# Attention with the fifth blocks of two heads in one transpose, 1/sum spread by transposes, and reordered maxima, products and table loads, in front of two gated layers on one core

## The chip, the cores and the metric

One core of a Trainium2 chip runs the whole program. The metric is device time in microseconds (us) of one execution; the programs are the kernel before the change and the kernel after it. The engines are named as the profile names them: PE (matmul) with PEld (its weight loads), DVE (vector), ACT (scalar activation), POOL (GpSimd), SP (which here only issues DMAs).

## The reference

Attention with rotated q and k over 2 batches, 8 heads, 576 positions and 64 dimensions, then two layers over 1152 tokens of 512, each with a hidden width of 2048, the first with ELU, the second with x·tanh(softplus(x)).

```python
q_rot, k_rot = (rotate(q), rotate(k))
scores = scale * np.matmul(q_rot, k_rot.transpose(0, 1, 3, 2))
scores = scores - np.max(scores, axis=-1, keepdims=True)
attn = np.exp(scores)
attn = attn / (np.sum(attn, axis=-1, keepdims=True) + 1e-09)
return np.matmul(attn, v).astype(np.float32)
...
h = x @ w_in
g = np.where(h > 0.0, h, alpha * (np.exp(np.minimum(h, 0.0)) - 1.0))
return (g @ w_out).astype(np.float32)
...
h = x @ w_in
sp = np.where(h > 20.0, h, np.log1p(np.exp(np.minimum(h, 20.0))))
g = h * np.tanh(sp)
return (g @ w_out).astype(np.float32)
```

## The kernel before

The 16 heads are handled as 8 pairs of heads, both heads of a pair side by side in the 128 partitions. A pair has nine score tiles of 128 query rows by 576 keys: tile i = 0..7 is head i mod 2, query rows 128·(i div 2) and on, and tile 8 holds the last 64 query rows of both heads. One step of the main loop is a unit u = 9p + i, and the order in which the loop body calls its parts is the order in each engine's queue (the schedule is by hand). The stages of a unit are spread over later units:

- `do_S` (L385): the scores into the double bank `ps_s` (two buffers), as products of values split into a rounded high part and a rest. In pairs 0 and 1 (`FLAT = 2`) the two heads of a double tile (units u and u+1, u even within the pair) are multiplied together in rows 0-63 and 64-127, and all of it is issued in the even unit. From pair 2 on each tile has its own four matmuls with stacked operands `ka`, `qa`, `qb`, which POOL splits (L298, L299) and SP copies into place (L323) during the pair before.
- `do_max` (L392, DVE) the row minimum of the negated scores; `do_exp` (L400, ACT) exp into the tile `P` (four buffers) with the row sum accumulated aside.
- `do_T`, three units later (`LAG`): four transposes of 128x128 into one of two banks `psT` (L441) and a fifth of the last 64 keys into `psL` (L442); `do_evac` (L455 on DVE, L457 on ACT) and `do_evac_last` (L467, DVE) bring them to `pt`, a tile with the five key chunks.
- `do_inverse` (L409 to L418, DVE): 1/sum of a group of tiles (group 0 is tiles 0 to 3, 256 query columns; group 1 is tiles 4 to 8, 320 columns), each widened to 64 columns; `do_spread` (L423, PE) turns it into a row layout in the bank `psA` by fp32 products with the identity; `do_keep` (L432, ACT) copies it to `R`.
- `do_av` (L473): five key chunks; in each, head 0 goes to output partitions 0-63 of `psA` and head 1 to 64-127, in fp32, which is two records per matmul in the trace. `do_x` (L488, DVE) multiplies by `R` and frees `psA`; `do_xh`, `do_xl` split the result into `XH` and `XL`, the operands of the first layer.

A table `plan` says in which unit each spread and product stands: the spread of group 0 in unit 6 of a pair, its products in units 7 and 9, the spread of group 1 in unit 11 (unit 2 of the next pair), its products in units 12 and 14. POOL rotates q and k of the pair after next (L273 to L277), and weights of the first layer are prepared in the last pairs (`weight_part`). After the last tile, `tail` puts first-layer products (L183, `g1_mm`) between the remaining steps. The layers that follow are a stream of matmuls on PE (L183, L683, L712).

In what follows, stage 1 is units 0 to 17 (pairs 0 and 1), stage 2 the units from 18 to 70, stage 3 the rest of attention with its tail, stage 4 the two layers. What one double tile does in stage 1, on each engine's queue, is

```python
do_S(u)            # even unit: both tiles
do_max(u)
do_T(u - LAG)
do_spread / do_av
do_evac(u - LAG)
do_exp(u)
```

so in the old order the maximum of tile u+1 stands on DVE behind the work of unit u.

## Time and profile before

| | us |
|---|---|
| runs, median of 3 | 574.96 |
| lowest, highest | 574.5, 1397.33 |
| the profiled execution's own time | 570.46 |
| its span, first to last instruction | 568.6 |

The profile is of one execution, so its rows add up to its own time, which is 4.5 us below the median. PE is busy 97% of the span and the granted clock is full (1.00) throughout. A row of the timeline gives the start within the span, the length, the engine, the line of the kernel, the operation, what it writes and reads, the shape, how many instructions were merged, and in brackets the engine's idle time before it and what ended it. The ends of matmuls are modelled, so the cost of a PE instruction in a dense stretch is read from start to start.

### The profile page before, as it was taken

The numbers are of one execution on the slowest core, as the hardware profiler recorded it, in microseconds if no ns is written. First come the engines' busy times: TensorE is split into PE (matmuls) and PEld (weight loads), VectorE is DVE, ScalarE is ACT, GpSimd is POOL, SyncE is SP. The second block draws the span as 40 slices with busy tenths as digits, with TensorE's granted clock in tenths as the row PEclk, the third lists the DMA queues.
The fourth block names the chain that finished last, engine by engine and source line by source line (L and its number), as shares of the span: only waits on it lengthen the run. The fifth ranks groups of instructions, "written<-read, shape, count | busy, mean of one in ns | idle before, by whom it ended". The sixth has DMA issues, their size and how long they took to land.

```text
span 568.6 us, 10131 instructions
## 1 busy us (share of the span) xinstructions
PE 553.9 (97%) x3888; PEld 499.7 (88%) x3888; DVE 376.9 (66%) x607; ACT 277.9 (49%) x512; POOL 238.7 (42%) x227
## 2 busy tenths in 40 slices
PE   7799999999999999999999999999999999999997
PEld 6568677777789999999999999999999998999985
DVE  6666899888846766777777777869844555432222
ACT  3646666667755665455555456435443322322110
POOL 6998999982310323323322331445533332230000
PEclk9999999999999999999999999999999999999999
DMA  6368676655110323223222322234532423000012
GB/s 231 110 197 258 205 228 178 184 143 161 38 39 4 108 80 107 76 76 96 91 74 78 108 75 75 85 115 139 159 116 84 121 88 110 22 14 10 29 65 93
DMA packets 43120, 60.69 MB, mean 107 GB/s; under 512 B 13760, under 2 KB 31936, under 8 KB 42304
## 3 DMA queue, kind: packets, MB, share of 16 engines
q1 hardware_dynamic: 42528, 59.46, 34.2%
q8 instruction: 31, 0.51, 0.4%
q10 hardware_dynamic: 544, 0.59, 0.3%
q14 instruction: 17, 0.14, 0.1%
HBM read 46.20 MB, written 2.36 MB: 85 GB/s over the span
## 4 chain that ended last, share of the span: by engine, by line
PE 85%; DVE 6%; ACT 3%; DMA 2%; issue 1%; POOL 1%; SPq 1%; ACTq 0%; POOLq 0%; DVEq 0%
PE ps_s L183 34%; PE ps_g L683 18%; PE ps_h L712 17%; PE ps_s L385 5%; PE psA L473 5%; PE psT L441 4%; DMA qk_t<-in_qk_dram 2%; PE psA L423 2%; DVE mn L392 1%; ACT P L400 1%; DVE wu L99 1%; PE psL L442 1%; DVE pt L455 1%; DVE R L488 0%; DVE rw L411 0%
## 5 line engine op out<-in xcount | busy, mean ns | idle before, releaser
L392 DVE TENSOR_REDUCE mn<-ps_s 128x1 f32<-128x576 f32 x72 | 53.9, 751 | 19.2 <-PE ps_s L385 15.2
L661 ACT ACTIVATE ta<-ps_s 128x576 f32<-128x576 f32 x32 | 20.8, 649 | 92.7 <-PE ps_s L183 92.6
L400 ACT ACTIVATE P<-ps_s,mn 128x576 f32<-128x576 f32 x72 | 53.1, 739 | 9.5 <-DVE mn L392 6.8
L183 PE MATMUL ps_s<-XH,wi0h 128*128 128x288 f32 x256 | 54.9, 296 | 0.9 <-DVE tb L218 0.9
L99 DVE TENSOR_SCALAR wu<-wu 128x512 int32<-128x512 int32 x64 | 33.7, 527 | 32.9 <-POOL wu L95 32.9
L183 PE MATMUL ps_s<-XL,wi0h 128*128 128x288 f32 x256 | 54.5, 294 | 0.0
L183 PE MATMUL ps_s<-XL,wi1h 128*128 128x288 f32 x256 | 54.4, 294 | 0.0
L183 PE MATMUL ps_s<-XH,wi0l 128*128 128x288 f32 x256 | 54.4, 294 | 0.0
L183 PE MATMUL ps_s<-XH,wi1l 128*128 128x288 f32 x256 | 54.2, 293 | 0.0
L183 PE MATMUL ps_s<-XH,wi1h 128*128 128x288 f32 x256 | 54.1, 293 | 0.0
L122 POOL TENSOR_TENSOR wi1l<-wu,wi1h 128x512 fp32r<-128x512 f32 x16 | 21.4, 1337 | 76.0 <-ACT wi1h L121 76.0
L122 POOL TENSOR_TENSOR wo0l<-wu,wo0h 128x512 fp32r<-128x512 f32 x16 | 21.9, 1366 | 68.3 <-ACT wo0h L121 56.4
L107 DVE SCALAR_TENSOR_TENSOR wu<-raw,wu 128x512 int32<-128x512 int32 x64 | 48.8, 762 | 1.7
L103 DVE SCALAR_TENSOR_TENSOR wu<-raw,wu 128x512 int32<-128x512 int32 x64 | 47.6, 744 | 2.0
L95 POOL TENSOR_SCALAR wu<-raw 128x512 f32<-128x512 f32 x64 | 45.1, 706 | 4.7
L473 PE MATMUL psA<-pt,v_t 128*64 128x256 f32 (+1 forms) x320 | 45.6, 416 | 0.6 <-ACT R L432 0.6
L122 POOL TENSOR_TENSOR wo1l<-wu,wo1h 128x512 fp32r<-128x512 f32 x16 | 22.0, 1375 | 57.2 <-ACT wo1h L121 56.9
L663 DVE TENSOR_TENSOR g<-ta,g 128x576 fp32r<-128x576 f32 x25 | 20.4, 817 | 36.4 <-ACT g L662 36.4
L183 PEld LDWEIGHTS ps_s<-XH,wi0h 128*128 128x128 f32 x256 | 41.4, 188 | 3.2 <-DVE tb L218 1.3
L457 ACT ACTIVATE pt<-psT 128x512 f32<-128x512 f32 x44 | 26.3, 597 | 36.4 <-PE psT L441 36.4
L441 PE MATMUL psT<-idn,P 128*128 128x128 f32 x288 | 43.4, 274 | 0.0
L183 PEld LDWEIGHTS ps_s<-XH,wi1h 128*128 128x128 f32 x256 | 41.8, 188 | 1.2
(146 smaller groups left out, 1409.6 us busy)
## 6 DMA issues: line engine op xcount, KB each, us to landing
raw<-in_w_in_dram SPq DMA_DIRECT2D x32, 512.0 KB, 3.7
raw<-in_w_out_dram SPq DMA_DIRECT2D x32, 512.0 KB, 3.3
qk_t<-in_qk_dram SPq DMA_DIRECT2D x6, 1152.0 KB, 7.2
qa<-qh SPq DMA_DIRECT2D x24, 144.0 KB, 2.6
v_t<-in_vp_dram SPq DMA_DIRECT2D x8, 320.0 KB, 4.3
out_dram<-Y SPq DMA_DIRECT2D x9, 256.0 KB, 2.0
ka<-kh SPq DMA_DIRECT2D x12, 144.0 KB, 2.5
ka<-kl SPq DMA_DIRECT2D x12, 144.0 KB, 2.6
```

Source lines behind the costliest of these rows:

```text
L95: nc.gpsimd.tensor_scalar(out=u, in0=high.bitcast(F32), scalar1=REBASE, scalar2=0.0, op0=ALU.mult, op1=ALU.add)
L99: nc.vector.tensor_scalar(out=ui, in0=ui, scalar1=3, scalar2=0x7FFFFFF8, op0=ALU.logical_shift_left, op1=ALU.bitwise_and)
L103: nc.vector.scalar_tensor_tensor(out=ui, in0=high, scalar=-0x80000000, in1=ui, op0=ALU.bitwise_and, op1=ALU.bitwise_or)
L107: nc.vector.scalar_tensor_tensor(out=ui, in0=low, scalar=29, in1=ui, op0=ALU.logical_shift_right, op1=ALU.bitwise_or)
L122: nc.gpsimd.tensor_tensor(out=lo, in0=u, in1=plain(hi), op=ALU.subtract)
L183: nc.tensor.matmul(o[:, j, :HS], lhsT=w[:, cc, :], rhs=x[:, b, cc, j * HS:j * HS + HS], start=(k == 0), stop=(k == 3 * NC - 1),)
L392: nc.vector.tensor_reduce(out=m, in_=psS[u][:, :, :HS], axis=AX.XY, op=ALU.min)
L400: nc.scalar.activation(out=P.rearrange("p (j n) -> p j n", j=2), in_=psS.pop(u)[:, :, :HS], func=AF.Exp, scale=-1.0, bias=mn_t.pop(u), acc ...
L441: nc.tensor.transpose(tv[:, c, :], P[:, c * 128:c * 128 + 128], idn)
L473: nc.tensor.matmul(o[64 * h:64 * h + 64, :n], lhsT=v_t[p][:, c, 64 * h:64 * h + 64], rhs=pt_t[g][:, h, c, :], start=(c == 0), stop=(c == 4),)
L683: nc.tensor.matmul(o[:, j, :HS], lhsT=w[:, e * 128:e * 128 + 128], rhs=gt[:, i, j * HS:j * HS + HS], start=(k == 0), stop=(k == 3 * GF - 1),)
L712: nc.tensor.matmul(o, lhsT=l, rhs=w, start=(k == 0), stop=(k == 3 * GF - 1))
```

## The change

Eleven edits. (1) Head 1's keys are taken in another order: its four whole transposes begin at key 64, so that the last 64 keys of head 0 and the first 64 of head 1 lie beside each other in a `P` that now holds two tiles, and one 128x128 transpose serves both. (2) `P` becomes two buffers of two tiles plus one for tile 8. (3) V of head 1 is loaded in the new key order in three pieces, head 0's in one, and a second copy `vb` in the old order for tile 8; the products of head 1 in group 1 are split into 64 and 256 columns. (4) The spread is done by transposes of `rw`, and tile 8's part by two 64-column matmuls with a broadcast operand, which removes two DVE instructions per pair. (5) In pairs 0 and 1 both maxima stand behind the double tile, and in even units the transposes stand ahead of it. (6) `do_x` of group 1 moves from the unit after its products to the end of their unit. (7) One low-part split and the copies of pair 0's last queries move to unit 2. (8) The last group's products go to `psT[0]`, and its `do_x` stands right behind them. (9) The first-layer product of step 4 goes to a bank pair of `ps_g`. (10) The second-layer products of the first block start one step later, and step 8 runs two. (11) The extra table load at the middle is dropped, and one weight job is opened at unit 19.

On PE, unit 20 (pair 2; `psT` and `psL` are transposes, `rw`, `idn_79` and `rc` belong to the spread of pair 1's group 1). Before:

```order
L385 MATMUL ps_s<-ka,qa 128x288 x2
L385 MATMUL ps_s<-ka,qb_113 128x288 x2
L441 MATMUL psT_82<-idn,P 128x128 x4
L442 MATMUL psL<-idn,P 64x128
L423 MATMUL psA<-idn,rw 128x128 x2
L423 MATMUL psA<-idn_79,rw 128x64
L385 MATMUL ps_s<-ka,qa 128x288 x2
```

and now, with the scores of unit 21 and the first products that follow (`vb_t` is the second copy of V):

```order
L471 MATMUL psL<-idn,P_599 64x128
L445 MATMUL psA<-idn,rw 128x128 x2
L449 MATMUL psA<-idn,rc 64x64 x2
L406 MATMUL ps_s<-ka,qa 128x288 x2
L406 MATMUL ps_s<-ka,qb_117 128x288 x2
L469 MATMUL psT_80<-idn,P 128x128 x4
L509 MATMUL psA<-pt_85,v_t 64x320
L509 MATMUL psA<-pt_85,vb_t 64x64
L509 MATMUL psA<-pt_85,v_t 64x256
```

The spread has two transposes and two 64-column matmuls, the tile in front of the products has no fifth transpose, and a chunk has three matmuls where it had two.

On DVE, units 4 to 7 of stage 1 (`mn` is the maximum, `rc` and `rw` the inverse sums, the copies are evacuations). Before:

```order
L392 TENSOR_REDUCE mn<-ps_s 128x1
L409 TENSOR_REDUCE rc<-sums_76 128x4
L410 RECIPROCAL rc<-rc 128x4
L411 TENSOR_REDUCE rw<-rc 128x256
L392 TENSOR_REDUCE mn<-ps_s 128x1
L455 COPY pt_85<-psT_81 128x4x128
L392 TENSOR_REDUCE mn<-ps_s 128x1
L467 COPY pt_85<-psL 64x2x256
L392 TENSOR_REDUCE mn<-ps_s 128x1
```

and now:

```order
L413 TENSOR_REDUCE mn<-ps_s 128x1 x2
L435 TENSOR_REDUCE rc<-sums_76 128x4
L436 RECIPROCAL rc<-rc 128x4
L437 TENSOR_REDUCE rw<-rc 128x256
L487 COPY pt_84<-psT_80 128x4x128
L413 TENSOR_REDUCE mn<-ps_s 128x1 x2
L499 COPY pl_86<-psL 128x256
```

The inverse no longer stands between the two maxima of units 4 and 5, nor the evacuation of the fifth blocks between those of 6 and 7.

On SP, the loads between the copies for pair 2 and those for pair 3 (`raw` are weights, `v_t` V of pair 2, `qk_t` q and k of pair 4). Before:

```order
L339 DMA bl_107<-ql 64x64
L77 DMA raw<-in_w_in_dram 128x4x256 x2
L265 DMA v_t<-in_vp_dram 128x640
L260 DMA qk_t<-in_qk_dram 128x2304
L323 DMA ka<-kh 64x576 x2
```

and now:

```order
L284 DMA vb_t<-in_vp_dram 128x5x64
L77 DMA raw<-in_w_in_dram 128x4x256 x2
L276 DMA v_t<-in_vp_dram 128x5x64
L277 DMA v_t<-in_vp_dram 64x5x64
L278 DMA v_t<-in_vp_dram 64x4x64
L279 DMA v_t<-in_vp_dram 64x64
L271 DMA qk_t<-in_qk_dram 128x2304
L342 DMA ka<-kh 64x576 x2
```

Four more issues stand in front of the load of pair 4 and of the copies for pair 3.

The diff, cut:

```diff
-    GB, GE, PB = 9, 2, 4
+    GB, GE, PB = 9, 2, 2
...
-        o = ps_s()
+        if (m, f, b) == (0, 0, 1):
+            o = g_pool[0].tile([128, 2, 512], F32, tag="g", name="ps_g", bufs=2)
+        else:
+            o = ps_s()
...
-            nc.sync.dma_start(out=v, in_=vp[p])
+            nc.sync.dma_start(out=v[:, :, 0:64], in_=vp[p, :, :, 0:64])
+            nc.sync.dma_start(out=v[0:64, :, 64:128], in_=vp[p, 64:128, :, 64:128])
+            nc.sync.dma_start(out=v[64:128, 0:4, 64:128], in_=vp[p, 0:64, 1:5, 64:128])
+            nc.sync.dma_start(out=v[64:128, 4, 64:128], in_=vp[p, 0:64, 0, 64:128])
...
+        def load_vb(p):
+            vb = att.tile([128, 5, 64], F32, tag="vb", name="vb_t", bufs=1)
+            nc.sync.dma_start(out=vb, in_=vp[p, :, :, 64:128])
...
-            for h in range(2 * g):
-                rows = slice(64 * h, 64 * h + 64)
-                nc.vector.tensor_reduce(
-                    out=rw[rows, 2, h, :], in_=r[rows, 4:5].to_broadcast([64, 64]).unsqueeze(2), axis=AX.X, op=ALU.add
-                )
...
-            for t in range(2 + g):
-                nc.tensor.matmul(
-                    psA[:, 128 * t:min(128 * t + 128, 256 + 64 * g)],
-                    lhsT=rw[:, t].rearrange("p h d -> p (h d)"), rhs=idn if t < 2 else idn2,
+            for t in range(2):
+                nc.tensor.transpose(
+                    psA[:, 128 * t:128 * t + 128], rw[:, 2 * t:2 * t + 2].rearrange("p h d -> p (h d)"), idn
+                )
+            for h in range(2 * g):
+                nc.tensor.matmul(
+                    psA[64 * h:64 * h + 64, 256:320],
+                    lhsT=r[:, 4:5].to_broadcast([128, 64]), rhs=idn[:, 64 * h:64 * h + 64], start=True, stop=True,
...
-            nc.tensor.transpose(psL[:S - 512, i % 4, :], P[:, 512:S], idn)
+            if i == TPP - 1:
+                nc.tensor.transpose(psL[:S - 512, 0, :], P[:, 512:S], idn)
+            elif i % 2:
+                P2 = P2_t.pop((p, i // 2)).rearrange("p h k -> p (h k)")
+                nc.tensor.transpose(psL[:, i // 2, :], P2[:, 512:640], idn)
...
+        def av_home(p, g):
+            return psT[0].rearrange("p c q -> p (c q)") if (p, g) == (NP - 1, 1) else psA
...
+                m = n if h == 0 else 256
+                v = v_t[p][:, c, 64 * h:64 * h + 64]
+                if h and g:
+                    w = slice(256, 320)
+                    rhs = pt_t[g][:, h, c, w] if c < 4 else pl_t[g][:, 320:384]
+                    part(h, w, vb_t[p][:, c, :], rhs, True)
+                rhs = pt_t[g][:, h, c, :m] if c < 4 else pl_t[g][:, :m]
+                part(h, slice(0, m), v, rhs, not (h and g))
...
+            both = u < FLAT * TPP and i < TPP - 1
+            first_T = both and i % 2 == 0 and u >= LAG
+            if first_T:
+                do_T(u - LAG)
...
-            if u < NU:
-                do_max(u)
+            for w in ((u, u + 1) if i % 2 == 0 else ()) if both else (u,):
+                if w < NU:
+                    do_max(w)
...
+            for (pp, g) in ends.get(u, []):
+                if g == 1 and pp < NP - 1:
+                    do_x(pp, g)
...
+            if u == 19:
+                open_job()
...
-                    pend.extend((n + (D1 if n < half - 1 else LATE[e]), (0, (g, b, e))) for e in range(NC))
+                    pend.extend((n + (2 if n < GF else D1 if n < half - 1 else LATE[e]), (0, (g, b, e))) for e in range(NC))
...
-            if n == half - 1:
-                nc.scalar.preload_act_table_set("mish")
```

## Rows read from the trace of the kernel before

**Rows 1.** Stretch, length, busy us of PE, PEld, DVE, ACT, POOL; clock, DMA.
```profile
0.00:46.80 46.80, 39.12 (x301) 30.53 (x302) 29.64 (x64) 24.41 (x55) 41.46 (x43) 1.00 0.55 173
46.80:153.00 106.20, 104.48 (x790) 79.98 (x787) 92.26 (x175) 72.32 (x170) 79.44 (x71) 1.00 0.63 182
...
175.60:568.60 393.00, 388.86 (x2640) 370.61 (x2640) 242.48 (x348) 168.66 (x264) 114.19 (x110) 1.00 0.27 83
```

**Rows 2.** Waits of PE, stages 1 to 3: total us, times, longest.
```profile
PE ps_s L385 <- ACT P L400: 5.3, 8, 1.1
...
PE psA L423 <- DVE R L488: 0.7, 1, 0.7
PE ps_s L385 <- ACT P L400: 0.6, 1, 0.6
...
PE ps_s L183 <- DVE tb L218: 0.7, 1, 0.7
PE psA L473 <- ACT R L432: 0.6, 1, 0.6
```

**Rows 3.** Timeline of stage 1: start, us, instruction, [idle before <-what ended it].
```profile
17.10 0.53 PE L385 MATMUL ps_s<-kh,qa 64*128 64x288 f32 x3 [0.33 <-ACT P L400]
...
18.07 0.76 DVE L392 TENSOR_REDUCE mn<-ps_s 128x1 f32<-128x576 f32 x1 [1.35 <-PE ps_s L385]
...
19.27 0.74 ACT L400 ACTIVATE P<-ps_s,mn 128x576 f32<-128x576 f32 x1
19.47 0.75 DVE L392 TENSOR_REDUCE mn<-ps_s 128x1 f32<-128x576 f32 x1
...
20.34 0.74 ACT L400 ACTIVATE P<-ps_s,mn 128x576 f32<-128x576 f32 x1 [0.24 <-DVE mn L392]
...
21.22 0.53 PE L385 MATMUL ps_s<-kh,qa 64*128 64x288 f32 x3 [0.67 <-ACT P L400]
```

**Rows 4.** Operands of pairs 2 and 3: issue, landing, first use; window 43:60.
```profile
39.90 1.18 SPq L323 DMA_DIRECT2D qb<-ql  x2
...
DMA to landing us min/median/max: 2.5/2.6/2.6
...
46.81 0.38 PE L385 MATMUL ps_s<-ka,qa 128*128 128x288 f32 x1
...
54.53 1.10 SPq L323 DMA_DIRECT2D qb<-ql  x2
...
DMA to landing us min/median/max: 5.3/5.4/5.4
...
65.95 0.51 PE L385 MATMUL ps_s<-ka,qa 128*128 128x288 f32 x2
...
43.00:60.00 17.00, 16.36 (x125) 12.36 (x124) 12.12 (x25) 10.37 (x25) 15.18 (x15) 1.00 0.86 245
```

**Rows 5.** Timeline of PE in stage 2: transposes, A·V and the spread.
```profile
111.45 0.60 PE L441 MATMUL psT<-idn,P 128*128 128x128 f32 x4
111.89 0.27 PE L442 MATMUL psL<-idn,P 128*64 128x128 f32 x1
112.09 1.84 PE L473 MATMUL psA<-pt,v_t 128*64 128x320 f32 x12
113.86 0.54 PE L385 MATMUL ps_s<-ka,qa 128*128 128x288 f32 x2
...
114.93 0.27 PE L442 MATMUL psL<-idn,P 128*64 128x128 f32 x1
115.32 0.71 PE L423 MATMUL psA<-idn,rw 128*128 128x128 f32 x4
115.79 0.52 PE L385 MATMUL ps_s<-ka,qa 128*128 128x288 f32 x2
```

**Rows 6.** Timeline of PE in stage 2: the spread of the second group.
```profile
106.68 0.78 PE L423 MATMUL psA<-idn,rw 128*128 128x128 f32 x6
107.27 0.51 PE L385 MATMUL ps_s<-ka,qa 128*128 128x288 f32 x2
```

More of the change, by code (lines that the diff above doesn't have):

```diff
@@ L188, in g1_mm @@
         return o
+    g_pool = [None]
     G = {}
@@ L195, in tmp, with tmps @@
     def tmp(tag):
+        return late_pool[0].tile([128, S], F32, tag=tag, name=tag, bufs=5)
+    def tmps():
         if tmp_pool[0] is not None:
-            return tmp_pool[0].tile([128, S], F32, tag="P", name="P", bufs=PB)
-        return late_pool[0].tile([128, S], F32, tag=tag, name=tag, bufs=5)
+            t = tmp_pool[0].tile([128, 2, S], F32, tag="P", name="P", bufs=PB)
+            return t[:, 0, :], t[:, 1, :]
+        return tmp("ta"), tmp("tb")
     def galloc(m, f, b):
@@ L487, in do_x @@
             x = R_t[p, g]
-            nc.vector.tensor_tensor(out=x, in0=psA[:, :(256, 320)[g]], in1=x, op=ALU.mult)
+            nc.vector.tensor_tensor(out=x, in0=av_home(p, g)[:, :(256, 320)[g]], in1=x, op=ALU.mult)
         def do_xh(p, g):
@@ L513, in attention @@
             nc.vector.memset(t[:, :, 1:2], 1e-9)
-        nc.vector.memset(rw[:, 2], 0.0)
-        nc.vector.tensor_tensor(out=idn2, in0=idn[:, 0:64], in1=idn[:, 64:128], op=ALU.add)
-        for t in pt_t:
-            nc.vector.memset(t[S - 512:128, :, 4, :], 0.0)
+        nc.vector.memset(pl_t[1][S - 512:128, 256:384], 0.0)
         for t in qb:
@@ L573, in attention @@
                     ends.setdefault(u, []).append((p, g))
-        for u in range(max(av_at) + 2):
+        for u in range(max(av_at) + 1):
             p, i = divmod(u, TPP)
@@ L590, in attention @@
             for (pp, g) in ends.get(u - 1, []):
-                do_x(pp, g)
-            if u < NU:
-                do_max(u)
+                if g == 0:
+                    do_x(pp, g)
+            for w in ((u, u + 1) if i % 2 == 0 else ()) if both else (u,):
+                if w < NU:
+                    do_max(w)
             if u == 1:
                 first_lo(*HEAD[3])
-            if 0 <= u - LAG < NU:
+            if u == 2:
+                first_lo(*HEAD[-1])
+                stack_q(0)
+            if 0 <= u - LAG < NU and not first_T:
                 do_T(u - LAG)
@@ L606, in attention @@
                     do_av(pp, g, c)
+                    if (pp, g, c) == (NP - 1, 1, 4):
+                        do_x(pp, g)
             if u >= NU:
-                tail(u - NU, False)
+                tail(u - NU, 0, None)
             if 0 <= u - LAG < NU:
@@ L753, in step @@
                 if m == 0:
-                    pend.extend((n + (D1 if n < half - 1 else LATE[e]), (0, (g, b, e))) for e in range(NC))
+                    pend.extend((n + (2 if n < GF else D1 if n < half - 1 else LATE[e]), (0, (g, b, e))) for e in range(NC))
                 else:
                     pend.extend((n + D2, (1, (g, t))) for t in TB[b])
-            cnt = 2 if n in (half - 2, half + 1, half + 2) or n > half and n % 8 == 4 else 1
+            cnt = 2 if n in (2 * GF, half - 2, half + 1, half + 2) or n > half and n % 8 == 4 else 1
             while pend and cnt and pend[0][0] <= n:
@@ L795, with tail @@
     early = {}
-    def tail(k, late):
-        if late:
-            if k in (2, 3):
-                elu_lo(*elu_hi(*early[k - 2]))
-                early[k - 2] = None
-            if k in (1, 2):
-                early[k - 1] = elu(0, k - 1, 0, early[k - 1])
-        elif k in (0, 1, 3):
-            n = min(k, 2)
-            early[n] = g1_mm(0, n, 0)
+    def tail(k, late, last_x):
+        if not late:
+            if k in (0, 1, 3):
+                n = min(k, 2)
+                early[n] = g1_mm(0, n, 0)
+        elif k == 1:
+            early[0] = elu_join(*elu(0, 0, 0, early[0]))
+        elif k == 2:
+            early[0] = elu_lo(*elu_hi(*early[0]))
+            early[1] = elu(0, 1, 0, early[1])
+        elif k == 3:
+            early[1] = elu_join(*early[1])
+            last_x()
+            early[1] = elu_lo(*elu_hi(*early[1]))
     with tc.tile_pool(name="att", bufs=1, reuse_waits="tile") as att, tc.tile_pool(
```

69 lines of the change are left out of this document (42 added, 27 removed).

## The prediction

> **What bounds the kernel now.** I read four views in this order. The windows by stage [rows 1] show PE busy for 39.1 of 46.8 us in stage 1, 104.5 of 106.2 in stage 2 and 388.9 of 393 in stage 4, at full clock: from stage 2 on the kernel is as long as the work in PE's queue, and DVE (92.3) and POOL (79.4 of 106.2) fit beside it. The waits of PE [rows 2] say where it idles: 5.3 us in stage 1, eight times for the exp that frees a score bank; 0.6 and 0.7 in stage 2; 0.6 and 0.7 in stage 3. The timeline of stage 1 [rows 3] shows why: one double tile takes 21.22 - 17.10 = 4.12 us, and its second maximum starts at 19.47, though the first ended at 18.83 and both tiles were there. The timeline of stage 2 [rows 5, 6] gives the price of each PE instruction from start to start. Stage 4 gets no new work, and its 393 us stay.
>
> **PE work per pair.** Transposes lie (111.89 - 111.45) / 4 = 0.11 us apart [rows 5]. Nine fifth-block transposes become five: 4 x 0.11 = 0.44 saved. A spread of 128 columns in fp32 is two records, 0.11 each: four records stand at 115.32, the six of the other group take 107.27 - 106.68 = 0.59 [rows 5, 6]. Group 0: two of four records go, 0.22 saved. Group 1: 0.59 becomes two transposes (0.22), plus two 64-column matmuls of two records, side by side in the two halves of the columns, 0.12, plus going into and out of the 64-column form. That change is in the trace: fifth transpose to A·V takes 112.09 - 111.89 = 0.20 where the next transpose would come after 0.11, so 0.09 each way [rows 5]. Together 0.52, 0.07 saved. The Trainium skill says the same against this edit (TensorEngine Tiling (Array Packing), Key Properties): a change of the tiling mode drains the engine. It gives no price; without the drain group 1's edit would save 0.25 instead of 0.07, and the sum would gain 1.4 us.
>
> A·V of group 1 gets five more matmuls per pair, of 64 columns; the columns per half stay 320. The row at 112.09 has 12 records of 320 columns in 113.86 - 112.09 = 1.77 us; at the spread's pace (0.59 us for 640 columns) they would need 3.5 one after another, so the heads run side by side. The split piece costs nothing if it streams in its half, 0.12 per chunk (two records of 0.06) if it streams alone. The nearest row is the packed one, so I take 0.03, 0.15 per pair; both ends, 0 and 0.6, stay in the range. Below nothing it can't go, as no column is saved.
>
> Net per pair: 0.44 + 0.22 + 0.07 - 0.15 = 0.58.
>
> **Stage 1.** A double tile now needs: start of the second tile's scores to the first maximum 0.97 (17.10 to 18.07), one maximum 0.76, then two exps of 0.74 [rows 3], as the second maximum ends while the first exp runs: 3.2, with handovers some 3.4 instead of 4.12, 0.7 for six doubles, 4.2. The first double has its maxima together already. From the waits: six of eight waits of 5.3 in all, 4.0. The transposes that now stand ahead of the scores fill PE while it waits, and free the exp from an evacuation in front of it. With 2 x 0.58 of PE work, 5.2 us are at stake. But unit 18 can't start earlier than its operands: the second copy of `qb` is issued at about 40.5 and lands 2.6 later, at 43.1, where PE uses it at 46.81 [rows 4]. POOL and SP set that, not PE; POOL is busy 41.5 of 46.8 [rows 1], and no edit shortens its chain. So the cap is 3.7; I take 3.5, with 1.5 as the low end.
>
> **Stage 2.** Six pairs' worth of PE work: 6 x 0.58 = 3.5. The waits of 0.6 and 0.7 [rows 2] go: they are one late exp and one late `do_x`, in the pair where two weight jobs open together, and one now opens two units earlier: 1.3. The spread of group 0 waits for `do_x` of group 1 also where the page of waits is too coarse: 114.93 to 115.32 is 0.39 instead of 0.11 [rows 5], in three pairs; with `do_x` a unit earlier that goes, 0.8. Against it stand the copies for pair 3. SP has four more issues in front of them and of the load of pair 4 (each about 0.59, as two take 1.18), 2.4 us, and the queues carry 160 KB more, in 256-byte pieces, in a stretch in which they are 86% busy at 245 GB/s [rows 4]. The bytes alone are 0.65 us; the pieces have no row, from 0 to 1.5. I take 1.0 in all. The last `qb` copy for pair 3 landed at 55.1 + 5.4 = 60.5 and would at 61.5. PE would be at unit 27 at 43.3 + (65.95 - 46.81) - 1.3 - 0.58 = 60.6: a new wait of 0.9. For later pairs I take the copies to be in time: PE waits for none of them now [rows 2], and the burst of two weights with a pair load comes once. Stage 2 gives 3.5 + 1.3 + 0.8 - 0.9 = 4.7.
>
> What else is queued. `do_x` waits on DVE for A·V, with a weight part and the next maximum behind it, and behind that maximum an exp and the score bank two units later; I take 0, as PE has a whole unit in between, with 0.3 in each of six pairs as the end. The exp of an even unit waits for the transposes of three units earlier, which now hold its two-tile buffer; they stand right behind the scores, four to five times 0.11, less than the maximum it waits for anyway. `vb` waits on SP for the last product of the pair before, with weights, V and the pair load behind it; that product is four units back. The two small reduces and the smaller fifth-block copies on DVE are hidden behind PE, and so is the table load on ACT: no saving, and no cost if DVE stays at 92 of 106.
>
> **Stage 3.** The last A·V no longer waits for the copy out of `psA` (0.6), though it still needs the last evacuation: 0.5. The first-layer product of step 4 has a bank of its own: 0.7 [rows 2]. **Stage 4.** Order only: 0, between -0.5 and 0.5.
>
> **Sum.** 3.5 + 4.7 + 1.2 = 9.4 us. The profiled execution took 570.46, which gives 561.1. The median is 574.96; with the same saving the forecast is 565.5, 1.6% less. About 2% is what a measurement of this kernel can tell from no change, so this is likely a gain within that bound.
>
> **Rivals.**
> *The cap binds on and off (569).* POOL and SP, not PE, set the start of each pair. POOL is busy 15.2 of 17.0 us in the window of [rows 4]; if each pair load comes 2.4 us later and POOL never catches up, stage 2 keeps 3.5 + 1.3 - 2.4, and stage 1 gives the low 1.5 to 2.5: about 6. For it: the 86% DMA share. Against: PE waits for no copy in stage 2 now [rows 2].
> *The pieces run in order (568).* The Trainium skill has it (TensorE: Matmul & The Clock Gate, Part 3, The mechanism) that matmuls start and end strictly in program order, tiles overlapping only with their neighbours in it. By the rows: a 320-column record takes 0.29, a 256 one 0.24, a 64 one 0.06; in order a chunk is 0.29 + 0.06 + 0.06 + 0.24 = 0.65 instead of 0.59, 40 x 0.06 = 2.4 us lost. The 12 records in 1.77 us fit six slots of two, where strict order of low and high passes would need seven; so the trace rather speaks against it.
> *The halves fall out of step (588).* The slower end. If three unequal matmuls per chunk stop the two heads from overlapping, group 1's chunk goes from 0.59 to 1.18: 40 x 0.59 = 23.6 us against 9.4 saved, 589. From 0.24 per chunk on it decides. For it: nothing in the trace packs unequal pieces. Against: both halves are addressed as before.
> *More comes (562).* No new wait at pair 3, the split piece free, the small stalls below the resolution of the waits gone: 0.9 + 1.2 + 1 more, 562.4.
>
> **How the numbers follow.** Forecast as worked out (563 to 567) 0.36; the cap 0.2; in order 0.12; out of step 0.07; more 0.25. The cap and in order stay within 2%, out of step is slower by over 2%, and over 2% faster means under 563.5, which holds for most of "more" and a small part of the forecast: 0.3. With another 0.02 for an unforeseen loss that is 0.3 / 0.61 / 0.09. The range runs from 560.5 (more, with the drain of the 64-column form at nothing) to 571 (the cap with both ends of the split piece), 8 in 10.
>
> **What would show it.** In the changed profile: the fifth-block transposes x40 instead of x72 and the spread's transposes one record each; double tiles of stage 1 about 3.4 us apart where no product stands between; unit 18 near 43.3 with a wait for a DMA or POOL just before; pair to pair in stage 2 shorter by 0.6 to 0.9 us; a 3-chunk product of group 1 at 1.8 to 1.9 us; no wait of step 4. It is wrong if A·V of group 1 takes over 2.5 us for three chunks, if waits for copies return in every pair, or if DVE makes PE wait in stage 2.

## The result and the profile after

| | before | after |
|---|---|---|
| runs, median (us) | 576.14 (574.5 to 1397.33) | 567.75 (567.34 to 569.35) |
| after / before, 95% interval | | 0.987 (0.983 to 0.991) |
| profiled execution, own time | 570.46 | 567.34 |
| its span | 568.6 | 565.5 |

The new kernel is 1.3% faster: the interval excludes no change, and the gain stays under 2%. The execution of 1397.33 us is left out of the ratio. The two profiles lie only 3.1 us apart, the medians 8.4 (7.2 from the median of 574.96 that the prediction started from). That gap is part of the result. The stages of the two profiles, cut at the same instructions (unit 18's scores, the last tile of the last pair, the end of the first layer's fifth block); columns: stretch, length, busy us of PE, PEld, DVE, ACT, POOL; clock, DMA share, GB/s. After:

```profile
0.00:45.94 45.94, 37.98 (x300) 30.17 (x301) 26.16 (x59) 23.99 (x55) 40.30 (x42) 1.00 0.60 175
45.94:147.19 101.25, 100.12 (x815) 81.08 (x813) 91.22 (x163) 71.89 (x170) 82.47 (x72) 1.00 0.78 202
147.19:171.48 24.29, 24.20 (x194) 22.46 (x194) 12.23 (x22) 14.98 (x28) 3.46 (x4) 1.00 0.11 35
171.48:565.50 394.02, 389.83 (x2618) 371.17 (x2616) 240.70 (x346) 165.04 (x260) 113.72 (x110) 1.00 0.27 83
...
200.00:250.00 50.00, 50.00 (x377) 50.00 (x376) 34.15 (x50) 26.57 (x43) 14.24 (x15) 1.00 0.24 75
```

Before, at the cuts that [rows 1] doesn't have:

```profile
46.81:153.04 106.23, 104.51 (x790) 79.97 (x788) 92.29 (x175) 72.36 (x170) 79.43 (x71) 1.00 0.63 182
153.04:178.98 25.94, 24.68 (x187) 21.94 (x185) 13.87 (x25) 15.03 (x28) 3.60 (x4) 1.00 0.07 22
178.98:568.60 389.62, 385.55 (x2618) 367.30 (x2616) 241.07 (x346) 166.06 (x260) 114.19 (x110) 1.00 0.27 84
...
200.00:250.00 50.00, 50.00 (x387) 50.00 (x386) 35.01 (x51) 28.66 (x47) 15.97 (x16) 1.00 0.27 85
```

| | forecast | measured |
|---|---|---|
| stage 1 | 3.5 | 46.81 - 45.94 = 0.87 |
| stage 2 | 4.7 | 106.23 - 101.25 = 4.98 |
| stage 3 | 1.2 | 25.94 - 24.29 = 1.65 |
| sum up to the fifth block | 9.4 | 7.50 |
| stage 4 | 0 | 389.62 - 394.02 = -4.40 |

Stage 4 runs the same 2618 records, and PE is busy 99% of it. Yet 50 us hold 387 of them before and 377 after: the stream itself is slower.

**Stage 1.** The waits of PE, to be read beside the 5.3 us in eight waits for exp of [rows 2] (columns: who waits for whom, us in all, times, longest):

```profile
PE ps_s L406 <- ACT P L426: 1.8, 4, 0.6
PE ps_s L406 <- ACT qa L321: 1.5, 1, 1.5
...
PE psA L509 <- ACT R L457: 1.2, 1, 1.2
PE psA L509 <- DVE pt L487: 1.1, 1, 1.1
PE psT L469 <- ACT pt L489: 0.5, 1, 0.5
PE psL L471 <- DVE pl L499: 0.3, 1, 0.3
```

The waits for exp fell from 5.3 to 1.8 as meant, but 3.1 came in that were not there, all for copies (the last four rows). The second row is the wait ahead of the first scores. It differs between executions, so stage 1 is better counted from there. The first scores before, and after:

```profile
9.33 0.74 PE L385 MATMUL ps_s<-kh,qa 64*128 64x288 f32 x4 [0.93 <-ACT qa L302]
...
9.84 0.73 PE L406 MATMUL ps_s<-kh,qa 64*128 64x288 f32 x4 [1.54 <-ACT qa L321]
```

From them to unit 18 the kernel before takes 46.81 - 9.33 = 37.48 us and the new one 45.94 - 9.84 = 36.10. So 1.38 us were gained, and 0.51 of it was lost again by the later start of this execution: in the seven profiles of this kernel and of those below with the same code ahead of the first scores, they start anywhere from 9.22 to 9.84. PE's busy time in the stage fell by 1.15, so the moved maxima and transposes as such brought some 0.2. Around the first of the new waits, the timeline:

```profile
22.22 0.68 ACT L329 ACTIVATE qa<-qk_t 128x576 fp32r<-128x576 f32 x1 [1.62 <-POOL qk_t L296]
22.81 0.58 ACT L489 ACTIVATE pt<-psT 128x512 f32<-128x512 f32 x1
...
23.29 0.38 ACT L457 ACTIVATE R<-psA 128x256 f32<-128x256 f32 x1
...
23.71 0.43 PE L509 MATMUL psA<-pt,v_t 128*64 128x256 f32 x1 [1.21 <-ACT R L457]
```

ACT stands 1.62 us for POOL's rotation of pair 1's q, with the evacuation and the copy of `R` queued behind it. And around the second:

```profile
33.18 1.42 DVE L413 TENSOR_REDUCE mn<-ps_s 128x1 f32<-128x576 f32 x2 [1.60 <-PE ps_s L406]
...
34.52 0.27 DVE L499 COPY pl<-psL 64x128 f32<-64x128 f32 x1
34.72 1.27 DVE L487 COPY pt<-psT 128x512 f32<-128x512 f32 x2
...
35.54 0.45 PE L509 MATMUL psA<-pt,v_t 128*64 128x320 f32 x1 [1.05 <-DVE pt L487]
```

DVE stands idle for 1.60 us, does both maxima, and only then the copies for which A·V waits.

**Stage 2.** A 3-chunk product of group 1 and a spread, which answer to [rows 5, 6]:

```profile
50.80 0.38 PE L445 MATMUL psA<-idn,rw 128*128 128x128 f32 x2
51.11 0.34 PE L449 MATMUL psA<-idn,rc 128*64 128x64 f32 x4
51.37 0.53 PE L406 MATMUL ps_s<-ka,qa 128*128 128x288 f32 x2
...
56.03 0.48 PE L509 MATMUL psA<-pt,v_t 128*64 128x320 f32 x1
56.03 0.33 PE L509 MATMUL psA<-pt,vb_t 128*64 128x64 f32 x2
...
57.82 0.40 PE L406 MATMUL ps_s<-ka,qa 128*128 128x288 f32 x1
```

The product takes 1.79 us (1.77 before), the spread 0.57 (0.59). The signs named in the prediction are there in part: fifth-block transposes x40 instead of x72, the product at 1.79, and pairs shorter by 0.66 to 0.80 us where three of them follow each other. From last tile to last tile (61.30, 78.32, 95.48, 112.60) three pairs take 17.02, 17.16 and 17.12 us, 17.82 each before; the one behind them takes 17.56, 17.44 before. What changed beside PE is POOL: it stands 4.23 us for the load of pair 4, and then it is full. The row of that wait, and one window of 17 us behind it, after:

```profile
57.50 1.42 POOL L292 TENSOR_TENSOR qk_t<-qk_t,tab 128x576 f32<-128x576 f32 x1 [4.23 <-DMA qk_t<-in_qk_dram]
...
78.00:95.00 17.00, 16.80 (x139) 13.67 (x137) 15.90 (x28) 11.74 (x29) 16.75 (x14) 1.00 0.82 219
```

And the same two before, where POOL had time left:

```profile
53.82 1.41 POOL L273 TENSOR_TENSOR qk_t<-qk_t,tab 128x576 f32<-128x576 f32 x1 [0.59 <-DMA qk_t<-in_qk_dram]
...
78.00:95.00 17.00, 16.88 (x131) 13.26 (x129) 15.28 (x29) 11.46 (x28) 15.66 (x14) 1.00 0.73 210
```

### The profile page after: what moved, and what is told of

It reads as the page before. It is cut to its first block, busy times and chain, and to the rows that moved or that the text cites. A ratio compares the mean times of both kernels' runs of the same rounds, so it can differ in the third digit from the quotient of the medians.

```text
span 565.5 us, 10181 instructions
## 1 busy us (share of the span) xinstructions
PE 552.1 (98%) x3920; PEld 504.9 (89%) x3920; DVE 370.3 (65%) x588; ACT 275.9 (49%) x511; POOL 240.0 (42%) x227
## 4 chain that ended last, share of the span: by engine, by line
PE 47%; issue 28%; POOL 15%; DVE 5%; DMA 2%; ACT 1%; SPq 1%; POOLq 0%; DVEq 0%; ACTq 0%
PE ps_h L772 17%; PE ps_s L186 15%; PE ps_s L406 5%; PE psA L509 5%; POOL wu L95 4%; PE psT L469 3%; POOL wi0l L122 2%; POOL wo1l L122 2%; POOL wi1l L122 2%; POOL wo0l L122 2%; DVE wu L107 1%; DMA qk_t<-in_qk_dram 1%; DVE mn L413 1%; POOL qk_t L296 1%; POOL qk_t L292 1%
## 5 line engine op out<-in xcount | busy, mean ns | idle before, releaser
L426 ACT ACTIVATE P<-ps_s,mn 128x576 f32<-128x576 f32 x72 | 53.1, 740 | 11.7 <-DVE mn L413 8.9
L186 PE MATMUL ps_s<-XH,wi0h 128*128 128x288 f32 x248 | 53.5, 297 | 0.1
L186 PE MATMUL ps_s<-XL,wi0h 128*128 128x288 f32 x248 | 53.1, 296 | 0.3 <-DVE XL L758 0.3
L186 PE MATMUL ps_s<-XH,wi0l 128*128 128x288 f32 x248 | 52.9, 295 | 0.0
L107 DVE SCALAR_TENSOR_TENSOR wu<-raw,wu 128x512 int32<-128x512 int32 x64 | 50.9, 795 | 1.7
L103 DVE SCALAR_TENSOR_TENSOR wu<-raw,wu 128x512 int32<-128x512 int32 x64 | 49.2, 768 | 1.9
L228 DVE SCALAR_TENSOR_TENSOR tb<-ta,tb 128x576 f32<-128x576 f32 x30 | 22.7, 757 | 33.4 <-ACT tb L224 33.1
L122 POOL TENSOR_TENSOR wi0l<-wu,wi0h 128x512 fp32r<-128x512 f32 x16 | 21.4, 1338 | 48.5 <-ACT wi0h L121 48.5
```

Of the source, the lines that this page charges most:

```text
L103: nc.vector.scalar_tensor_tensor(out=ui, in0=high, scalar=-0x80000000, in1=ui, op0=ALU.bitwise_and, op1=ALU.bitwise_or)
L107: nc.vector.scalar_tensor_tensor(out=ui, in0=low, scalar=29, in1=ui, op0=ALU.logical_shift_right, op1=ALU.bitwise_or)
L122: nc.gpsimd.tensor_tensor(out=lo, in0=u, in1=plain(hi), op=ALU.subtract)
L186: nc.tensor.matmul(o[:, j, :HS], lhsT=w[:, cc, :], rhs=x[:, b, cc, j * HS:j * HS + HS], start=(k == 0), stop=(k == 3 * NC - 1),)
L426: nc.scalar.activation(out=P.rearrange("p (j n) -> p j n", j=2), in_=psS.pop(u)[:, :, :HS], func=AF.Exp, scale=-1.0, bias=mn_t.pop(u), acc ...
```

## The experiments

**The kernel before, once more** (no edit).

> The kernel before, unchanged, profiled a second time. In its first profile the first layer's matmuls of 288 columns stood 130 ns apart (alternating 132 and 128) from 182 to 354 us, in the profile of the kernel after 133.2 ns apart (131, 131, 131, 140) over the same steps, though both run the same products there. Theory A (two rhythms of the stream, which one an execution falls into is not fixed by the kernel, and the first profile caught the quick one): this execution, or most of the timed ones, show the slow one, a span near 573 us and times near 574.5 to 575; if the profiled one is slow, its records stand 133 ns apart from 180 to 350 us. Theory B (the order of the kernel before gives the quick rhythm always, and the change lost it): 130 ns again from 182 us, a span of 568.6 and times near 570.5. In both the attention part ends where it ended: last fused tile at 153.0, step 4's product at 175.7.

Median 575.91, ratio to the kernel before 1.001 (0.998 to 1.005); the profiled execution took 574.59, its span is 572.7:

```profile
178.80:572.70 393.90, 389.71 (x2617) 371.07 (x2616) 241.38 (x346) 165.91 (x260) 114.33 (x110) 1.00 0.26 83
200.00:250.00 50.00, 50.00 (x378) 50.00 (x377) 34.95 (x51) 27.43 (x44) 16.07 (x16) 1.00 0.27 85
```

Theory A: stage 4 takes 393.90, as in the kernel after (394.02), and unit 18, the last tile and step 4 stand within 0.25 us of the first profile. So the first profile of before had caught the stream at 130 ns, and 4.3 us of its time are the execution's, not the kernel's.

**Extra matmuls in the stream.**

```diff
+        if n in NUDGE:
+            nc.tensor.matmul(
+                o[:, 0, HS:HS + NUDGE[n]], lhsT=hi[:, 0, :], rhs=XH[:, b, 0, 0:NUDGE[n]],
+                start=True, stop=True, skip_group_check=True,
+            )
```

> The kernel after with one extra matmul of 16, 32, 48 ... 224 columns into unused columns of the score bank ahead of twelve of the first layer's blocks, one width per block; the outputs don't change. If the rhythm of the stream is a matter of phase (Theory A), some of the widths tip it into the quick one: stretches between two such blocks then read 130 ns per matmul and others 133, and the stretch stays as it is until the next extra matmul; each nudge costs 0.03 to 0.1 us, some 0.8 in all, against 4.2 us if the whole half were quick. If the pace is set by something beside PE's queue (weights being prepared, transfers), the extra matmuls change nothing: 133 ns throughout, and about 0.8 us more than the kernel after.

568.54. After eleven of twelve widths the stream ran at 133 ns, after the one of 32 columns (second row) at 130.0 until the next one:

```profile
187.70:200.70 13.00, 13.00 (x100) 13.00 (x98) 10.29 (x15) 9.09 (x15) 5.85 (x6) 1.00 0.37 123
200.70:213.29 12.59, 12.59 (x99) 12.59 (x98) 7.02 (x11) 6.97 (x11) 2.22 (x3) 1.00 0.19 50
213.29:226.19 12.90, 12.90 (x100) 12.90 (x99) 8.28 (x13) 7.55 (x12) 4.07 (x5) 1.00 0.30 90
```

So an extra matmul can tip the pace, and the new pace lasts until the next one. That the width or a phase decides it is argued, not shown.

**That width alone**, at blocks 5, 13 and 21.

> The kernel after with an extra matmul of 32 columns ahead of the first layer's blocks 5, 13 and 21 alone. In the kernel with twelve widths the one of 32 was followed by 96 matmuls at 130.0 ns and every other width by 133 to 134. Theory A (phase: this width at this place tips the stream into the quick rhythm, and without another extra matmul it stays): 130 ns from about 174 us until the next nudge or the wait near 350, 1300 matmuls by 3.1 ns, 4 us less, a span near 562 and times near 564; should the next nudge tip it back, the stretches alternate and half of that is gained. Theory B (chance): the stretches show 133, as in most executions, and the time is that of the kernel after, 567.5 to 568.

565.63 to 569.74, median 567.06. The first left the stream at 133, the second tipped it to 130.0 (229 to 279 us), the third tipped it back. What this run shows beside that is in stage 2, whose code is that of the kernel after: the last pair's last tile stands at 150.54 instead of 147.19, as PE waits for copies:

```profile
63.65 0.51 PE L413 MATMUL ps_s<-ka,qa 128*128 128x288 f32 x2 [0.96 <-DMA qa<-qh]
64.54 0.40 PE L413 MATMUL ps_s<-ka,qb 128*128 128x288 f32 x1 [0.38 <-DMA qb<-ql]
83.02 0.51 PE L413 MATMUL ps_s<-ka,qa 128*128 128x288 f32 x2 [1.10 <-DMA bh<-qh]
84.11 0.40 PE L413 MATMUL ps_s<-ka,qb 128*128 128x288 f32 x1 [0.59 <-DMA qb<-ql]
```

POOL had stood 6.42 us for the load of pair 4 here. The supply of copies is at its edge: the profile of the kernel after shows no such wait, this one 3.0 us.

**Edit 5 alone undone.**

```diff
-            both = u < FLAT * TPP and i < TPP - 1
-            first_T = both and i % 2 == 0 and u >= LAG
+            both = first_T = False
```

> The kernel after with edit 5 alone undone: in pairs 0 and 1 each maximum stands in its own unit again and the transposes behind the scores. The new order was predicted to be worth 2.4 of stage 1's 3.5 us (the rest is PE work). Theory A (the waits only moved, from the scores waiting for exp to A.V and the transposes waiting for copies): unit 18 starts at 45.7 to 46.5, within 0.6 of the 45.94 of the kernel after, with some 5 us of waits for exp back. Theory B (the new order does pay, and something else in stage 1, the later start above all, ate it): unit 18 at 48 or later.

Unit 18 at 48.90, but the granted clock was 0.57 in the mean from 18 to 26 us, so that the number says nothing. Pair 1 lies behind that at full clock: from last tile to last tile it takes 20.06 us, 19.78 in the kernel after, 20.46 before. There the new order is worth 0.28 us, and with the old one PE waits 2.0 us for exp and 0.2 for `R` instead of 0.5 for exp and 1.4 for copies. So in pair 1 the waits only moved, as theory A has it; pair 0 is left open.

**Stage 1 mended.**

```diff
+            if first_T:
+                evac_all(u - LAG)
...
+            if u == 4:
+                second_split(2)
+            if u == 10:
+                do_x(0, 0)
...
-            if u in (3, 5):
-                second_split(2 if u == 3 else 0)
...
+            if u == 7:
+                second_split(0)
                 stack_q(1)
```

`evac_all` is a unit's evacuations in their old order; here they stand ahead of both maxima. The split of pair 1's k on ACT and one `do_x` follow behind a unit's evacuations; the split of its q moves from unit 5 to the end of unit 7. One rotation on POOL moves with it (not shown).

> The kernel after with three moves in stage 1: the copies out of the transposes' banks stand ahead of both maxima in units whose transposes come first (and the last one of group 1 ahead of do_x in unit 10); the high part of pair 1's q moves on ACT from the end of unit 5 to the end of unit 7, behind the copies of R and the two exps, with one rotation on POOL ahead of its low part; that of k moves behind the copy of unit 4. Theory A (1.21 us at 23.71 is ACT standing for 1.6 us on POOL's rotation of q with the copies queued behind it, 1.05 at 35.54 and 0.29 at 31.64 are copies behind two maxima on DVE): these three waits fall to under 0.3 each, unit 18 starts between 43.7 and 44.6, where the second qb copy (landing near 44 to 45) may hold it. Theory B (PE is held by something else, e.g. the exps, and the wait comes back at the next scores): unit 18 at 45.5 to 46.2.

The three waits are gone (one of 0.08 is left), and pair 1 takes 18.68 us instead of 19.78. Unit 18 starts at 45.10, later than expected, as the granted clock fell to 0.50 here too:

```profile
8.00:10.00 2.00, 0.71 (x8) 0.57 (x10) 1.27 (x3) 0.64 (x2) 1.87 (x4) 1.00 1.00 405
...
14.00:16.00 2.00, 2.00 (x12) 1.72 (x11) 1.24 (x2) 1.03 (x2) 1.92 (x3) 0.50 0.03 8
```

What was gained was lost at unit 27, where PE stands 1.29 and 0.42 us for pair 3's copies (the profile puts the first down to an ACT instruction long done; the same wait in the run with one width alone names the copy). The last pair's last tile came 1.4 us later than in the kernel after.

**More warm-up.** `WARM = 24` instead of 20.

> The kernel after with 24 instead of 20 warm-up matmuls ahead of the first scores, eight records and some 0.9 us more at full speed. In the profile of the kernel after PE stood 1.54 us before the first scores and the clock stayed at 1.00; in two of three kernels built on it PE stood 1.64 and 1.72 there and the granted clock was 0.50 from about 11.7 to 18 us, in the third it was 0.50 from 19 to 26 after a wait of 1.51. Theory A (the wait at the start, longer than the 0.4 and 0.9 of the two profiles of the kernel before, is what lets the clock fall): PE stands under 1.0 there, the clock stays at 1.00, pair 0's last tile starts at 24.8 or earlier, and the times lie within 0.5 us of the kernel after's 567.75, with the first scores no later than 9.9. Theory B (the clock falls by chance, whatever stands there): dips come as before, and nothing is gained.

Median 568.22. In the profile PE doesn't stand ahead of the first scores any more, and the clock stays at 1.00; unit 18 starts at 45.46. The last tile of the last pair, though, comes at 147.85, after a wait of 0.66 at 78.99 (which the profile puts down to POOL). Over all profiles: of the five in which PE stood 1.41 to 1.72 us ahead of the first scores, three show a granted clock of 0.50 later, two of them from 11.7 us on and one from 18, right behind a second wait of 1.51; of the nine with 0.99 or less, none. What such a fall costs hangs on what else holds PE. From the first scores to the last tile of pair 0, the first kernel with extra matmuls takes 15.76 us and the kernel after 14.96, so 0.8 more, as the wait of 1.21 for `R` didn't come in it. The mended kernel above, in which that wait is gone anyway, takes 15.77, and the next one, whose clock stays at 1.00, 13.38: 2.4 more, nearly all of it in one double tile (6.10 instead of 3.78).

**Mended, with weights loaded early.**

The mended stage 1 with these edits, and with `WARM = 24`:

```diff
-            if u == 16:
+            if u == 6:
                 prefetch_weights(2)
...
+            if u == 6:
+                prepare(1, 2)
+                second_split(0)
                 stack_q(1)
+                prepare(1, 3)
```

> The mended stage 1 once more, with pair 1's q split on ACT right behind the exp of unit 6 (POOL stood 1.64 us for it when it came after unit 7), with the two weight loads that stood in front of pair 3's copies on SP issued at unit 6, where the queues are all but idle, and with 24 warm-up matmuls. In the first mended kernel unit 18 came 0.8 earlier than in the kernel after in spite of the clock at 0.50 for six us, and then PE stood 1.29 and 0.42 at unit 27 for pair 3's copies, so that the last pair began 1.4 later. Theory A (stage 1's waits are mended, and what holds PE next is SP's supply of copies): with the clock at 1.00 unit 18 starts at 43.5 to 44.4, the wait at unit 27 falls under 0.5, and the last tile of the last pair starts at 145.0 to 146.0 instead of 147.19. Theory B (the supply is short whatever the order, as the queues carry the same bytes): the wait at unit 27 stays at 1 us or more, and the last pair starts at 146.8 or later.

565.74. Unit 18 starts at 43.21, 2.73 us earlier than in the kernel after (2.25 earlier than with the longer warm-up alone), and the waits of PE in stage 1 from the first scores on are 2.5 us, all for exp. Nothing waits at unit 27, but 0.65 us do at pair 4, and the last pair's last tile stands at 145.61, as theory A has it.

**One thing per pair.**

```diff
-        if (m, f, b) == (0, 0, 1):
+        if False:
...
+                if (p, g) in ((3, 1), (4, 0)):
+                    nc.tensor.matmul(
...
+                        rhs=idn, start=True, stop=True,
+                    )
+                    continue
...
+            if 41 <= u <= 49 and i % 2 == 0 and i < TPP - 1:
+                nc.tensor.transpose(psL[:S - 512, (1, 1, 2, 3)[i // 2], :], P[:, 512:S], idn)
...
-                if h and g:
+                if h and g and p != 2:
```

> The kernel after with one thing altered per pair, read from the time between the last tiles of neighbouring pairs (17.02, 17.16 and 17.12 us in the kernel after for 2 to 3, 3 to 4 and 4 to 5). Pair 2: the 64-column products of the second copy of V are left out (tile 8 of head 1 in pair 2 isn't computed). If the split piece is free, the period stays within 0.05; by the term of the prediction it shrinks by 0.15, and by 0.6 if the pieces stream alone. Pair 3 (with the first group of 4): the four transposes of 1/sum as fp32 products with the identity again; by the rows 0.44 more, under 0.2 if they hide. Pair 4 to 5: four fifth-block transposes put back for their time alone (they go to slots that are overwritten): 0.44 more by the rows, less if PE had slack there. In stage 3 the product of step 4 goes back to the scores' bank: the wait for DVE of 0.66 comes back in front of it, and its block starts 0.6 to 0.7 later against the last pair's start (21.09 us in the kernel after).

The periods are 17.10, 17.43 and 17.53 us. Pair 2: leaving the pieces out saves 0.03 and 0.04 in the two parts of the product (1.22 and 1.76 us against 1.25 and 1.80), nothing in the period (17.02 in the kernel after); they are all but free. Pair 3: the spread grows from 0.71 to 1.17 us by start-to-start distances, 0.46, but the period by 0.27 only. Pair 4: 0.41 more, of which 0.20 is a new wait of PE. In step 4, 0.63 us of waiting come back. This execution also fell into the 130 ns rhythm, and its 565.70 comes from there: its last pair stands 0.7 later than that of the kernel after.

**V in one piece.**

```diff
-            nc.sync.dma_start(out=v[:, :, 0:64], in_=vp[p, :, :, 0:64])
...
+            nc.sync.dma_start(out=v, in_=vp[p])
```

> The kernel after with V loaded in one piece per pair, as before (the second copy stays). The key order of head 1's V is then the old one, so that the output of head 1 isn't the reference's; all work is the same. In the kernel after and three kernels with the same order in stage 2, POOL stands for 4.2 to 6.4 us near 53 to 59 us until the load of pair 4 lands, which SP issues at 48.1 to 48.9 (before: 45.4, POOL idle 0.6); from there POOL is busy 16.7 of 17 us per pair, has no lead left, and PE waits for copies in some executions and not in others (nothing in the profile of the kernel after, 2.8 us at units 27 and 36 in another with the same attention). Theory A (the three further issues and the small pieces of V in front of that load are what takes POOL's lead): the load is issued 2.0 to 2.6 earlier against unit 18, POOL stands under 3 us for it, and PE has no wait for copies over 0.2. Theory B (the load comes late because the queues are full of weights and copies): POOL stands 4 us or more as before.

565.34. The load of pair 4 is issued at 45.91, 0.7 us after unit 18 instead of 2.2, so 1.4 earlier (2.0 to 2.6 expected), and POOL stands 1.95 us for it. PE has no wait for copies, and a pair takes 16.72 us:

```profile
54.67 1.41 POOL L289 TENSOR_TENSOR qk_t<-qk_t,tab 128x576 f32<-128x576 f32 x1 [1.95 <-DMA qk_t<-in_qk_dram]
...
60.55:77.27 16.72, 16.72 (x139) 13.65 (x137) 14.19 (x28) 11.87 (x29) 16.48 (x15) 1.00 0.79 226
```

PE is busy all the time and POOL 16.48 of 16.72. So 16.72 is what PE's work of a pair takes, and POOL's work is almost as long: before, it had 17.82 for it. The waits come out as theory A has them, with less of an earlier load than it said. It is one execution, but another one fits: with edit 5 undone PE reached unit 18 three us later, POOL stood 2.96 instead of 4.23 us, and with V in pieces the pairs that take 17.02 and 17.16 in the kernel after took 16.72 and 16.85.

**The next pair's load first**, on top of the mended kernel with early weights.

```diff
-                if p + 1 < NP:
+                if p + 1 < NP and p <= 2:
                     load_pair(p + 1)
...
+            if i == 5 and 1 <= p < NP - 3:
+                load_pair(p + 3)
```

> The second mended kernel (565.74 in its one run, with the slow rhythm in the layers), and the load of q and k of the pair after next issued from unit 14 on at the sixth unit of a pair, ahead of V's pieces and weights, instead of behind them. In the second mended kernel POOL still stood 0.8 and 2.45 us for such loads, and PE 0.55 and 0.65 in pair 4. Theory A (POOL and its loads are what bounds stage 2 once stage 1 is mended): POOL stands under 0.6 for them, each pair of stage 2 takes 16.8 to 17.1 us, the last tile of the last pair starts at 143.9 to 144.9 (145.61 there, 147.19 in the kernel after); times 564 to 565 with the slow rhythm, 560 with the quick one, 0.5% to 0.8% below the kernel after. Theory B (POOL has no time left whatever comes early): the last pair starts at 145.4 or later.

Median 565.43 (565.27 to 565.71), 0.981 of before (0.978 to 0.983). POOL stands for no load any more, but the last tile is at 145.50 only: the second copy of V, behind that load on SP, costs 0.92 us at 51.51. That is theory B's number (145.4 or later), yet pairs behind the first take 16.92 to 17.18: A's bound on POOL's loads is half right.

**The same with extra matmuls** at blocks 5 and 13.

> The same with extra matmuls of 32 columns ahead of the first layer's blocks 5 and 13. In the kernel with three of them the first left the stream at 133.3 ns, the second tipped it to 130.0 and the third tipped it back. Theory A (the same place tips it in every execution): 130 ns from block 13 (about 222 us) to 350, 960 matmuls by 3.3 ns, 3 us less than the kernel without, in the median. Theory B (which rhythm follows depends on phases that differ from run to run): the profile shows either, and the medians of the two kernels lie within 1 us.

Median 563.62 (562.51 to 566.4), 0.978 of before (0.975 to 0.981). In the profile the first tipped the stream to 130 and the second tipped it back, the reverse of the earlier run. So the same place doesn't tip it the same way each time, against theory A; but the median is 1.8 us lower, more than the 1 us of theory B, and that this is chance is not shown.

**Both corrected**: the second copy ahead of the load, one extra matmul at block 5.

> The third mended kernel (565.43 in the median, 565.27 to 565.71) with two corrections. There the second copy of V of pair 1, needed at 51.5 us, stood on SP behind the early load of pair 4 and landed 0.92 us late; now it is issued ahead of that load. And one extra matmul of 32 columns ahead of the first layer's block 5 alone: of the 32-wide ones met by the stream at 133 ns three of four were followed by 130, of those met at 130 both were followed by 133, so a second one is left out. Theory A: the wait at 51.5 goes, the last tile of the last pair starts at 144.0 to 144.8 (145.50 there), and with the slow rhythm the times lie at 564.3 to 564.8, with the quick one (from 172 to 350 us, 4 us less) near 560.5; the median of the executions under 562.5 if the one extra matmul mostly tips the stream, 564 or more if it mostly does not. Theory B (the 0.92 us come back at the next copies): the last pair starts at 145.2 or later.

561.61 to 567.18, median 564.96. The wait at 51.5 is gone and others came (1.18 at 56.32, put down to exp, and 0.69 at 77.61), the last tile stands at 145.78: theory B. The profiled stream stayed at 133. The steadiest version is thus the one with the load first, without extra matmuls: its slowest execution (565.71) is faster than the fastest of the kernel after (567.34).

## Why the prediction was right, and where its steps failed

The time was forecast as 565.5 within 560.5 to 571, a gain within 2%; 567.75 and 1.3% came. The range and the likeliest verdict hold. The likeliest single case (563 to 567) was just missed, and the time lies where "in order" (568) and the cap (569) were put, though neither is what this profile shows. Two terms of the sum were off in opposite directions, and it came out at 7.50 instead of 9.4.

**Stage 1 (3.5, measured 0.87, or 1.38 counted from the first scores): the step that failed.** "3.2, with handovers some 3.4 instead of 4.12" did come true where no product stands between (double tiles start at 16.75 and 19.93, 3.18 apart; 16.38 and 20.15 before). What failed is "six of eight waits": I asked what waits for exp, not what the two maxima and the earlier transposes put behind themselves. Of 4.0 us only 0.4 came (3.5 less for exp, 3.1 more for copies): the waits moved to A·V and the transposes. The mended kernels show it: with those copies moved ahead and ACT's split behind, pair 1 takes 18.66 to 18.68 us instead of 19.78, and unit 18 starts at 43.21, close to the "near 43.3" of the forecast (the longer warm-up alone brings 0.48 of the 2.73 us). The cap by copies was not reached in the kernel after: they landed at 43.24, and PE came at 45.94.

**PE's work per pair (0.58) was too small.** From start-to-start distances of PE's records between the last tiles of pairs 2 and 3 (us, idle time left out), beside the kernel with V in one piece, where PE waits for nothing:

| | before | V in one piece | forecast change |
|---|---|---|---|
| transposes | 5.31 | 4.59 | -0.44 |
| spread | 1.06 | 0.71 | -0.29 |
| A·V | 5.45 | 5.50 | +0.15 |
| scores | 5.89 | 5.91 | 0 |

The fifth blocks gave 0.72: I priced one at 0.11, like a whole transpose. With four put back the transposes of a pair take 5.22, 0.63 more than 4.59, so 0.16 each. That would be a price for the 64-column form, which the prediction had put on the spread (0.09 each way) but not here; the runs don't show it apart. The spread gave 0.35, the split cost 0.05. Together 1.02.

**The rivals "in order" and "out of step" didn't come.** (The sum of the second gives 589; its heading has 588.) The pieces of 320 and of 64 columns start together (56.03), the second record of the 320 starts at 56.35, behind the first of the 256 (56.20), and the product takes 1.79 us. By the prediction's rows strict order would cost 0.06 us a chunk; the row shows 0.01. The Trainium skill (TensorE: Matmul & The Clock Gate, Part 3, The mechanism) has matmuls start and end strictly in program order; by the starts of their records these two-record matmuls interleave instead.

**Stage 2 (4.7, measured 4.98)** is right by errors that offset each other: PE's busy time fell by 104.51 - 100.12 = 4.39 instead of 3.5, its idle time only from 1.72 to 1.13. From last tile to last tile the gains are 2.42 us in the first pair, where the two waits lay, then 0.80, 0.66, 0.71, -0.12 and 0.51. So a part of the 1.02 per pair did not arrive. In the three pairs where POOL is full, 16.72 became 17.02 to 17.16 (stalls of some 0.1, too short for the page of waits, stand ahead of their last tiles). In the one of 17.56, 0.40 is a wait of A·V for `R`; the rest is open. The 0.8 for the spread was too large, as PE stood 0.12 there and not 0.28. The wait at unit 27 (0.9) did not come in this profile, but by a hair. Its last copies, and their use:

```profile
L342 SPq DMA_DIRECT2D qb<-ql x2: 582/684/785, 58.1 to 58.9; - x2
...
DMA to landing us min/median/max: 4.1/4.3/4.4
...
63.01 0.43 PE L406 MATMUL ps_s<-ka,qb 128*128 128x288 f32 x2
```

They landed at 63.0 where 61.5 was forecast: the term of 1.0 for the copies was 2.7. PE, late from stage 1, reached unit 27 at 62.66 instead of 60.6 and used the last copy at 63.01. The wait did come where PE was earlier (1.29) and where the copies were later (0.96). So the rival "the cap binds on and off" lives in this kernel from execution to execution. By the run with V in one piece, its further issues and small pieces cost POOL the lead that it had.

**Stage 3 (1.2, measured 1.65)** as forecast: no wait of step 4, and 0.09 instead of 0.59 ahead of the last product; the rest, 24.68 - 24.20 = 0.48, is PE work, which I left out here.

**Stage 4 (0).** The work is the same, the rhythm was not. Subtracting from the median of the runs instead of from the profile's own time kept this out of the forecast; that was luck, as the prediction gave no reason for the 4.5 us between them, most of which the pace of this stage explains (4.3).

## What to carry to other kernels

When an order is changed to shorten one wait, list for each engine what now stands behind the moved instructions, and who needs it next; an engine that waits for its operand (here ACT for POOL) with short copies behind it is the first place to look. A saving on the bounding engine is worth its face value only as far as the suppliers have time left: compare their busy time per period with the new period, not with the old one. And before two profiles are subtracted, compare the pace of a stretch that the change doesn't touch.

## What the hardware showed that was not expected

A dense stream of matmuls of 288 columns has two stable paces: 132 and 128 ns in turn, mean 130.0, or 131, 131, 131 and 140, mean 133.3. Each lasted over 150 us, and a disturbance (an extra matmul, or a wait of 0.10 to 0.19 us near 350) can tip it either way, but doesn't always: of five extra matmuls of 32 columns that met the slower pace, three tipped it. Over the first layer this is 4.3 us, over half of what this change gave. What selects it was not found. The Trainium skill (TensorE: Matmul & The Clock Gate, Wait — 56ns, not 53.3ns?) gives, for back-to-back matmuls at full clock, the column count at 2.4 GHz and about 2.5 ns, by estimate 122.5 here; neither pace agrees (each matmul of this stream also has a weight load, 2616 for 2618).

The other surprise is the clock: where PE stood 1.4 to 1.7 us ahead of the first scores, three of five profiles show some six to eight us at a granted clock of 0.50 (the lower of its levels, 1.2 of 2.4 GHz) within nine us, the other two none, though the code ahead of the first scores is the same. By the first two mended kernels, one such fall cost some 2.4 us.
